# Output and slope rows by one generator, turned loads of d h behind the loads of h, and a scratch row moved, in a kernel for an S4 convolution with a gated feed-forward and its gradients

## The chip, the cores and the metric

The kernel runs on one core of a Trainium2 chip. The metric is the device time of one execution in microseconds (us). The engines of the core run side by side, each with its own list of instructions: TensorE (PE, matmuls; PEld is its weight load), VectorE (DVE), ScalarE (ACT), GpSimd (POOL) and SyncE (SP). SP here issues nearly all loads and part of the stores, POOL issues most of the other stores, and ACT a few. A DMA waits on its issuing engine until what it needs is there, so a DMA that must wait holds up every later one of the same engine.

## What is computed

With L = 2048 rows, D = 512 columns, F = 1792 hidden units and N = 128 states, in bf16:

```python
xn = layernorm(x)                       # over the 512 columns
K  = real(sum_n C[d,n] * exp(dt*A)[d,n]^l * dt*B[d,n])
s  = irfft(rfft(xn, 2L) * rfft(K, 2L))[:L] + xn * Dskip
h  = xn @ w1;   z = silu(h) @ w2;   g = silu(z)
out = x + s * g
```

Wanted are `out` (out_0) and the gradients for a given gradient r of `out`: of x (out_1), of A, B, C (real and imaginary, out_2 to out_7), of log_dt and Dskip (out_8, out_9), of w1 (out_10) and of w2 (out_11). The backward needs, row by row, d z = r * s * silu'(z) (called the slope rows here, kept in `k.do`), then d a = d z @ w2^T, d h = d a * silu'(h), the part of d xn that comes from d h @ w1^T (called Pd), d w2 = silu(h)^T d z, d w1 = xn^T d h, and at the end the backward of the norm, which adds Pd, the convolution's part dU and r.

## The kernel before

Everything is cut in blocks of 128 x 128. The 2048 rows are 16 tiles, and a *chunk* is two of them, 256 rows. The convolution goes through a Fourier transform made of matmuls, in four blocks of 128 columns. What doesn't stay on the chip goes to DRAM scratch and comes back: `Sd` the rows of s (one block of columns after the other), `Gd` the gate g, `Hd` the rows of h (turned: hidden units on the partitions), `DHd` the same for d h, `Ud` and `KXd` spectra, `Pd`, `dUd`.

The work is written as Python generators, and the order in which they are advanced is the order of the program. There are these stages:

1. Norm, tables and the forward of the convolution beside the feed-forward (`chain`, `gen_ffn_fwd`).
2. A stretch whose order for PE, ACT and DVE is written by hand as a string of letters. Among them G makes the gate rows and stores them to Gd, W makes the turned weights (`W1`, `W2`), L and M make the slope rows of chunks 0 and 1 (`gen_slope_rows(..., True)`). After it, "BB A BB A" begins the backward.
3. `paced(bwd, woven([ffb, out], [2, 1]), BR)`: the backward of the convolution (`gen_conv_bwd`, by columns, with the spectra as `sp_in` of 1 MB), and beside it two steps of `gen_ffn_da` for one of `gen_out`. This and all that follows is ordered by a scheduler; buffers (`bufs=`) and order decide what waits.
4. The gradients of the states (`gen_ssm_bwd`; loads `YT`, `Eb`, `GE`, `par_*`; tiles `ps_v`, `psS`, `gout`) beside the rest of `gen_ffn_da`, and then beside `gen_dw2`.
5. `interleave([gen_ln_bwd, dw])`: the backward of the norm beside the rest of `gen_dw2` and `gen_dw1`.

What the change touches, and the names to follow:

- `gen_ffn_da`, for each chunk: load h in two halves (`dhT`, of 8 and 6 hidden blocks, from Hd) and put silu' over it at once (ACT, L962); d z turned (`doT`); seven groups of 8 matmuls (`ps_da`, L989) with the product on DVE (L991); the store of d h to DHd (SP, L994); then `ps_dx` (L1000) with the copy to `pd_s` by ACT and its store to Pd (SP, L1003). At f == 2 it asks for slope rows two chunks ahead (`k.slopes`, `k.later`).
- The slope rows of chunks 2 to 7: a second instance of `gen_slope_rows` in a pool of its own ("late"), with loads of Sd (`S`) and of r (`Gs`), a silu' on ACT (L675) and two products on DVE (L678, L680).
- `gen_out`, chunks 0 to 7: loads of Sd (`go_s`) and Gd (`go_g`) two chunks ahead, a load of x (`go_x`, L707) in the chunk's own step, the products L709 and L710 on DVE, the store of out_0 by POOL.
- `gen_dw2`, for each of 14 hidden blocks: load `h_in` (128 x 2048, 512 KB, L1012; two buffers), turn it on PE (`pt_t`, L112; 16 matmuls), silu on ACT to `a_tok` (L1017), 16 matmuls `ps_w2` (L1032), copy to `o11` and store.
- `gen_dw1`, for each of 7 pairs of hidden blocks: two transposing DMAs of DHd to `dh_tok` (512 KB each, L1045; three buffers of a pair each), 4 x 16 matmuls `ps_w1` (L1050), copy to `o10` and store. In the profile `ps_w1` and `ps_w2` are both called ps_w, and o1, o10 and o11 are called o. As the buffers of dh_tok are free early, the scheduler puts the first six of its transposes on SP among the loads of `gen_dw2` and of the states.
- `gen_ln_bwd`, for each chunk: loads `du`, `pd_l`, `Gt` (SP, L1069 to L1073; four buffers), sums on DVE (L1082, and L1083 which writes its product to a scratch row `jk`), ACT, and `o1` (L1093, L1094), stored by POOL to out_1.

## Time and profile before

| | |
|---|---|
| Median of 3 runs | 687.6 us (687.19 to 688.8) |
| Profiled execution, its own time | 690.33 us |
| Span in its profile, first to last instruction | 688.4 us |
| Mean granted TensorE clock | 0.958 |
| Busy: PE, DVE, ACT | 600.2, 515.4, 455.3 us |
| DMA | 148.41 MB, mean 216 GB/s |

The profile has a page and views of the trace. In a timeline a row is: start in us, duration, engine, line, operation, output <- input by the program's names, shape, count (consecutive instructions are grouped), and in brackets the engine's idle time ahead of it with what ended it. A row of waits is: engine, what waited, what for, the sum in us, the number of times, the longest. A row of windows is: the stretch, then busy time of PE, PEld, DVE, ACT, POOL (with instructions), the granted clock of TensorE as a share of full speed, the mean busy share of the 16 DMA engines, and GB/s. SPq is SP's queue. A time comes from one execution, so it is compared with that execution's own time.

### The profile page before, as it was taken

The numbers are of one execution on the slowest core, as the hardware profiler recorded it, in microseconds if no ns is written. First come the engines' busy times: TensorE is split into PE (matmuls) and PEld (weight loads), VectorE is DVE, ScalarE is ACT, GpSimd is POOL, SyncE is SP. The second block draws the span as 40 slices with busy tenths as digits, with TensorE's granted clock in tenths as the row PEclk, the third lists the DMA queues.
The fourth block names the chain that finished last, engine by engine and source line by source line (L and its number), as shares of the span: only waits on it lengthen the run. The fifth ranks groups of instructions, "written<-read, shape, count | busy, mean of one in ns | idle before, by whom it ended". The sixth has DMA issues, their size and how long they took to land. (4 is left out here: it accounts for less than half of the span.)

```text
span 688.4 us, 14482 instructions
## 1 busy us (share of the span) xinstructions
PE 600.2 (87%) x5884; PEld 436.6 (63%) x5884; DVE 515.4 (75%) x917; ACT 455.3 (66%) x613; POOL 86.4 (13%) x172
## 2 busy tenths in 40 slices
PE   0687998999999977889789999989989969999798
PEld 0445665776675755657475866757677747766677
DVE  6979999899695789887687959537596753945880
ACT  6869779997969777857465775515677744634431
POOL 2354101010100120000000000000002020023211
PEclk9989999999999999899899999999999998999989
DMA  9955556846566787789777446469999996344994
GB/s 287 341 151 211 196 167 250 285 171 230 176 232 226 280 270 264 240 256 304 222 224 231 147 161 203 134 138 235 242 230 243 199 239 184 97 156 158 271 253 119
DMA packets 158018, 148.41 MB, mean 216 GB/s; under 512 B 79552, under 2 KB 134592, under 8 KB 154368
## 3 DMA queue, kind: packets, MB, share of 16 engines
q1 hardware_dynamic: 148640, 124.67, 63.6%
q0 software_dynamic: 6768, 19.93, 8.0%
q10 hardware_dynamic: 2544, 2.88, 1.3%
q8 instruction: 46, 0.75, 0.5%
q14 instruction: 20, 0.16, 0.1%
HBM read 65.01 MB, written 62.00 MB: 185 GB/s over the span
## 5 line engine op out<-in xcount | busy, mean ns | idle before, releaser
L45 ACT CAST dA<-ps_s 128x1024 bf16<-128x1024 f32 x89 | 87.2, 1031 | 10.0 <-PE ps_s L301 6.7
L832 DVE TENSOR_TENSOR Tp<-Vb,Eb 128x1344 bf16<-128x1344 bf16 x64 | 52.1, 854 | 25.7 <-issue 11.1
L989 PE MATMUL ps_da<-doT,W 128*128 128x256 bf16 x448 | 64.8, 288 | 3.2 <-DVE dhT L991 3.2
L615 PE MATMUL ps_o<-W,aT 128*128 128x512 bf16 x224 | 59.5, 396 | 5.5 <-ACT aT L607 3.2
L599 PE MATMUL ps_h<-XT,W 128*128 128x256 bf16 x448 | 61.7, 281 | 1.4 <-ACT hT L45 0.6
L45 ACT CAST dB<-ps_i 128x1024 bf16<-128x1024 f32 x47 | 46.0, 1032 | 23.0 <-PE ps_i L341 23.0
L341 PE MATMUL ps_i<-I,sp_in 128*128 128x256 bf16 x384 | 51.3, 281 | 8.8 <-DVE sp_in L374 4.7
L991 DVE TENSOR_TENSOR dhT<-ps_da,dhT 128x512 bf16<-128x512 f32 x56 | 38.0, 686 | 27.2 <-PE ps_da L989 20.8
L1050 PE MATMUL ps_w<-dh_tok,xn 128*128 128x256 bf16 x448 | 52.1, 281 | 4.0 <-DMA dh_tok<-DHd 4.0
L45 ACT CAST o<-ps_w 128x256 bf16<-128x256 f32 (+1 forms) x42 | 18.4, 442 | 54.4 <-PE ps_w L1050 23.9
L1000 PE MATMUL ps_dx<-W,dhT 128*128 128x512 bf16 x224 | 54.2, 383 | 0.0
L989 PEld LDWEIGHTS <-W 128*128 128x128 bf16 x448 | 44.3, 104 | 15.2 <-issue 7.9
L45 ACT CAST Vb<-ps_v 128x672 bf16<-128x672 f32 x64 | 42.4, 725 | 15.2 <-PE ps_v L822 15.2
L1032 PE MATMUL ps_w<-YD,a_tok 128*128 128x512 bf16 x224 | 52.3, 379 | 0.0
L1050 PEld LDWEIGHTS <-xn 128*128 128x128 bf16 x448 | 45.0, 101 | 11.2 <-issue 4.5
L599 PEld LDWEIGHTS <-W 128*128 128x128 bf16 x448 | 42.8, 101 | 13.7 <-issue 6.8
L341 PEld LDWEIGHTS <-sp_in 128*128 128x128 bf16 x384 | 36.9, 100 | 21.9 <-DVE sp_in L374 7.7
L301 PEld LDWEIGHTS <-TF 128*128 128x128 bf16 x384 | 27.1, 103 | 20.9 <-issue 13.9
L615 PEld LDWEIGHTS <-aT 128*128 128x128 bf16 x224 | 20.6, 101 | 30.4 <-issue 8.0
L46 DVE COPY dB<-pt_f 128x2048 bf16<-128x2048 bf16 x24 | 28.5, 1219 | 12.9 <-PE pt_f L310 12.7
L1000 PEld LDWEIGHTS <-dhT 128*128 128x128 bf16 x224 | 21.6, 99 | 22.6 <-issue 2.0
L45 ACT CAST hT<-ps_h 128x512 bf16<-128x512 f32 x56 | 32.3, 613 | 4.5 <-PE ps_h L599 4.5
(231 smaller groups left out, 1283.5 us busy)
## 6 DMA issues: line engine op xcount, KB each, us to landing
Yd<-YD SPq DMA_DIRECT2D x8, 1024.0 KB, 4.3
sp_in<-Ud SPq DMA_DIRECT2D x8, 1024.0 KB, 7.4
h_in<-Hd SPq DMA_DIRECT2D x14, 512.0 KB, 5.1
Ed<-E SPq DMA_DIRECT2D x8, 672.0 KB, 3.6
Eb<-Ed SPq DMA_DIRECT2D x8, 672.0 KB, 5.4
Hd<-hT POOLq DMA_DIRECT2D x8, 512.0 KB, 5.6
Ud<-dA SPq DMA_DIRECT2D x4, 1024.0 KB, 4.8
KXd<-dA SPq DMA_DIRECT2D x4, 1024.0 KB, 5.4
```

The costliest lines, as they stand in the source:

```text
L45: return self.nc.scalar.copy(out=out, in_=in_)
L46: return self.nc.vector.tensor_copy(out=out, in_=in_)
L301: nc.tensor.matmul(out=ps[:, j], lhsT=k.TF[:, 8 * h + j, c, :], rhs=U(8 * h + j), start=True, stop=True)
L341: nc.tensor.matmul(out=ps[:, g], lhsT=Y[:, c, g0 + g, :], rhs=k.I2[:, c].rearrange("p c m -> p (c m)"), start=(c == 0), stop=(c == 1))
L599: nc.tensor.matmul(out=ps[:, j], lhsT=k.W1[:, dk, ft * P:ft * P + P], rhs=XTv[:, :, dk, :], start=(dk == 0), stop=(dk == DK - 1))
L615: nc.tensor.matmul(out=ps[:], lhsT=aT[:, ft, t * P:t * P + P], rhs=k.W2[:, ft, :], start=(ft == 0), stop=(ft == FT - 1))
L832: k.nc.vector.tensor_tensor(out=Tp[:, c, :, r ^ c].rearrange("p e (q w) a -> p q w e a", w=2), in0=Vb[:, :, c].rearrange("p q w (e a) -> p ...
L989: nc.tensor.matmul(out=ps[:, j], lhsT=k.W2[:, ft, dk * P:dk * P + P], rhs=dTv[:, :, dk, :], start=(dk == 0), stop=(dk == DK - 1))
L991: nc.vector.tensor_tensor(out=dh[:, i0:i0 + 2, :], in0=ps[:], in1=dh[:, i0:i0 + 2, :], op=ALU.mult)
L1000: nc.tensor.matmul(out=ps[:], lhsT=dhs[ft // 8][:, ft % 8, t * P:t * P + P], rhs=k.W1[:, :, ft * P:ft * P + P], start=(ft == 0), stop=(ft ...
L1032: nc.tensor.matmul(out=ps[:], lhsT=at[:, t, :], rhs=k.do[:, t, :], start=(t == 0), stop=(t == k.T - 1))
L1050: nc.tensor.matmul(out=ps[:], lhsT=k.xn[:, t, dk * P:dk * P + P], rhs=dh[:, t].rearrange("p j n -> p (j n)"), start=(t == 0), stop=(t == k ...
```

## The change

- The slope rows of chunks 2 to 7 move from the late `gen_slope_rows` into `gen_out`, in a pool of its own ("go"). One load of Sd (`go_s`) serves slope and output of a chunk. r is loaded as `go_r`, x as `go_x` in three buffers and two chunks ahead with the others. The chunks go 2 to 7, then 0 and 1, and `gen_out` is finished ahead of the states' gradients.
- In `gen_ffn_da` the silu' of dhT is issued apart from its load, at f == 2 and f == 6; the check on slope rows moves from f == 2 to f == 4; pd_s gets two buffers.
- In `gen_dw1` the transposes of dh_tok are issued behind the last load of h_in. In the changed program all six first ones stand in a row on SP, behind that load and ahead of the loads of the norm.
- The scratch row jk moves from the norm's pool to the pool of the weights' gradients. o11 gets three buffers, o1 four.

In the changed program's own order, further: five loads of dhT stand on SP ahead of the spectra and the first loads of `gen_out`, with three silu' of dhT among ACT's copies of the turned weights; DVE does slope and output of chunks 4 and 5 one after the other; the last two turns and four of dw2's blocks of 16 matmuls remain on PE behind the last h_in load's release, with the states' psS matmuls ahead of it (before, two rounds of psS stood behind it).

```diff
@@ gen_slope_rows @@
-def gen_slope_rows(k, pool, chunks, early):
+def gen_slope_rows(k, pool, chunks):
...
-        n = 3 if early else 4
...
-        if early:
-            Gr = k.Gr[:, ts, :]
-        else:
-            G = pool.tile([P, 2, k.D], BF16, name="Gs", tag="Gs", bufs=2)
-            nc.sync.dma_start(G[:], k.g_v[:, ts, :])
-            Gr = G[:]
...
-def gen_out(k, pool):
+def gen_out(k, pool, early):
 
     nc = k.nc
     TT = nc.vector.tensor_tensor
@@ -696,21 +683,40 @@
         ts = slice(2 * c, 2 * c + 2)
         S = pool.tile([P, 4, 2, P], BF16, name="go_s", tag="go_s", bufs=2)
         nc.sync.dma_start(S[:].rearrange("p b t d -> p b (t d)"), k.Sd[:, :, 256 * c:256 * c + 256].rearrange("b p n -> p b n"))
+        G = None
+        if c >= early:
+            G = pool.tile([P, 2, k.D], BF16, name="go_r", tag="go_r", bufs=2)
+            nc.sync.dma_start(G[:], k.g_v[:, ts, :])
         g = pool.tile([P, 2, k.D], BF16, name="go_g", tag="go_g", bufs=2)
         nc.sync.dma_start(g[:], k.Gd[:, ts, :])
-        return S, g
-    q = [load(0), load(1)]
-    yield
-    for c in range(n):
-        S, g = q.pop(0)
-        x = pool.tile([P, 2, k.D], BF16, name="go_x", tag="go_x", bufs=1)
-        nc.sync.dma_start(x[:], k.x_v[:, 2 * c:2 * c + 2, :])
+        x = pool.tile([P, 2, k.D], BF16, name="go_x", tag="go_x", bufs=3)
+        nc.sync.dma_start(x[:], k.x_v[:, ts, :])
+        return S, G, g, x
+
+    def slope(c, G):
+        if G is not None:
+            with k.tc.issue_after(k.mark):
+                nc.scalar.activation(out=k.do[:, 2 * c:2 * c + 2, :], in_=k.do[:, 2 * c:2 * c + 2, :], func=ACT.Derivative_silu)
+    q = [load(early), load(early + 1)]
+    yield
+    slope(early, q[0][1])
+    order = list(range(early, n)) + list(range(early))
+    for i, c in enumerate(order):
+        S, G, g, x = q.pop(0)
+        yield
+        if G is not None:
+            o = k.do[:, 2 * c:2 * c + 2, :]
+            TT(out=o, in0=o, in1=G[:], op=ALU.mult)
+            TT(out=rows(o), in0=rows(o), in1=S[:], op=ALU.mult)
+            k.slopes = c + 1
+        if q:
+            slope(order[i + 1], q[0][1])
         yield
         TT(out=rows(g[:]), in0=rows(g[:]), in1=S[:], op=ALU.mult)
         TT(out=x[:], in0=x[:], in1=g[:], op=ALU.add)
         k.st(k.o0_v[:, 2 * c:2 * c + 2, :], x[:])
-        if c + 2 < n:
-            q.append(load(c + 2))
+        if i + 2 < n:
+            q.append(load(order[i + 2]))
         yield
 
 
@@ -959,12 +965,15 @@
         c, f0, n = halves[i]
         dh = da.tile([P, n, 256], BF16, name="dhT", tag="dhT%d" % n, bufs=3 if n == 8 else 2)
         nc.sync.dma_start(dh[:, 0:n], k.Hd[f0:f0 + n, :, 256 * c:256 * c + 256].rearrange("f p n -> p f n"))
-        nc.scalar.activation(out=dh[:, 0:n], in_=dh[:, 0:n], func=ACT.Derivative_silu)
         return dh
+
+    def slope(dh):
+        nc.scalar.activation(out=dh[:], in_=dh[:], func=ACT.Derivative_silu)
     for c in range(T // 2):
         if c == 0:
             dN = turned_rows(k, da, k.do, 0, "doT", k.evb)
             ahead = [load(0)]
+            slope(ahead[0])
             yield
         dT = dN
         dTv = dT[:].rearrange("p (t k) n -> p t k n", k=DK)
@@ -976,11 +985,13 @@
                 i = 2 * c + f // 4 + 1
                 if i < len(halves):
                     ahead.append(load(i))
-            if f == 2:
+            if f == 4:
                 while k.slopes < min(c + 3, T // 2):
                     next(k.later)
             if f == 4 and c + 1 < T // 2:
                 dN = turned_rows(k, da, k.do, c + 1, "doT", k.evb)
+            if f in (2, 6) and ahead:
+                slope(ahead[0])
             i0 = 2 * (f % 4)
             ps = k.pf.tile([P, 2, 256], F32, name="ps_da", tag="pf")
             for j in range(2):
@@ -994,7 +1005,7 @@
                 nc.sync.dma_start(k.DHd[f0:f0 + n, :, 256 * c:256 * c + 256].rearrange("f p n -> p f n"), dh[:, 0:n])
             yield
         for t in range(2):
-            pd = da.tile([P, D], BF16, name="pd_s", tag="pd_s", bufs=1)
+            pd = da.tile([P, D], BF16, name="pd_s", tag="pd_s", bufs=2)
             ps = k.pf.tile([P, D], F32, name="ps_dx", tag="pf")
             for ft in range(FT):
                 nc.tensor.matmul(out=ps[:], lhsT=dhs[ft // 8][:, ft % 8, t * P:t * P + P], rhs=k.W1[:, :, ft * P:ft * P + P],
@@ -1009,7 +1020,7 @@
 
     def load(ft):
         h = fw.tile([P, k.T, P], BF16, name="h_in", tag="h_in", bufs=2)
-        nc.sync.dma_start(h[:].rearrange("p t n -> p (t n)"), k.Hd[ft])
+        k.h_in = nc.sync.dma_start(h[:].rearrange("p t n -> p (t n)"), k.Hd[ft]).ins
         return h
 
     def turn(h):
@@ -1030,7 +1041,7 @@
         ps = k.pf.tile([P, k.D], F32, name="ps_w2", tag="pf")
         for t in range(k.T):
             nc.tensor.matmul(out=ps[:], lhsT=at[:, t, :], rhs=k.do[:, t, :], start=(t == 0), stop=(t == k.T - 1))
-        ob = fw.tile([P, k.D], BF16, name="o11", tag="o11", bufs=2)
+        ob = fw.tile([P, k.D], BF16, name="o11", tag="o11", bufs=3)
         k.evb(ob[:], ps[:])
         k.st(k.outs[11][ft * P:ft * P + P, :], ob[:])
         yield
@@ -1041,8 +1052,9 @@
     o10 = k.outs[10].rearrange("(k p) f -> p k f", p=P)
     for f in range(k.FT // 2):
         dh = fw.tile([P, k.T, 2, P], BF16, name="dh_tok", tag="dh_tok", bufs=3)
-        for j in range(2):
-            nc.sync.dma_start_transpose(dh[:, :, j, :], k.DHd[2 * f + j])
+        with k.tc.issue_after(k.h_in):
+            for j in range(2):
+                nc.sync.dma_start_transpose(dh[:, :, j, :], k.DHd[2 * f + j])
         ob = fw.tile([P, k.DK, 256], BF16, name="o10", tag="o10", bufs=2)
         for dk in range(k.DK):
             ps = k.pf.tile([P, 256], F32, name="ps_w1", tag="pf")
@@ -1078,9 +1090,8 @@
         m = lw.tile([P, 2, 4], F32, name="m", tag="m", bufs=2)
         for i in range(2):
             t = 2 * c + i
-            jk = lw.tile([P, D], BF16, name="jk", tag="jk", bufs=1)
             STT(out=cols(pd[:, i]), in0=cols(pd[:, i]), scalar=1.0, in1=du[:, :, i, :], op0=ALU.mult, op1=ALU.add, accum_out=m[:, i, 0:1])
-            STT(out=jk[:], in0=pd[:, i], scalar=1.0, in1=k.xn[:, t, :], op0=ALU.mult, op1=ALU.mult, accum_out=m[:, i, 1:2])
+            STT(out=k.jk[:], in0=pd[:, i], scalar=1.0, in1=k.xn[:, t, :], op0=ALU.mult, op1=ALU.mult, accum_out=m[:, i, 1:2])
         STT(out=m[:, :, 2:4], in0=m[:, :, 0:2], scalar=-1.0 / D,
             in1=k.rstd[:, 2 * c:2 * c + 2].unsqueeze(2).to_broadcast([P, 2, 2]), op0=ALU.mult, op1=ALU.mult)
         for i in range(2):
@@ -1088,7 +1099,7 @@
         return pd, Gt, m
 
     def rows(c, pd, Gt, m):
-        o1 = lw.tile([P, 2, D], BF16, name="o1", tag="o1", bufs=2)
+        o1 = lw.tile([P, 2, D], BF16, name="o1", tag="o1", bufs=4)
         for i in range(2):
             STT(out=o1[:, i], in0=k.xn[:, 2 * c + i, :], scalar=m[:, i, 3:4], in1=Gt[:, i], op0=ALU.mult, op1=ALU.add)
         TT(out=o1[:], in0=o1[:], in1=pd[:], op=ALU.add)
@@ -1225,7 +1236,7 @@
     k.g, k.mark = [], None
     early = range(2)
     streams = {"C": gen_conv_fwd(k, 3), "F": ffn, "G": gen_gate_rows(k, gp), "H": gen_ds_rows(k), "B": bwd,
-               "W": chained([gen_turned(k, k.W1, evw), gen_turned(k, k.W2, evw)]), "L": gen_slope_rows(k, gp, early[0:1], True), "M": gen_slope_rows(k, gp, early[1:], True)}
+               "W": chained([gen_turned(k, k.W1, evw), gen_turned(k, k.W2, evw)]), "L": gen_slope_rows(k, gp, early[0:1]), "M": gen_slope_rows(k, gp, early[1:])}
     ordered = ctx.enter_context(ExitStack())
     ordered.enter_context(tc.manual_schedule(engines={mybir.EngineType.PE, mybir.EngineType.Activation, mybir.EngineType.DVE}))
     for s in "GGG F GG F WWW CC W G C W C C W C HH GG C W C CC F C G L CC W C G HH L CC WW L HH C MM WW C L C HH WW MM".replace(" ", ""):
@@ -1238,25 +1249,25 @@
     turn = itertools.chain(["w8"] * 2, itertools.cycle(["w8"] * 2 + ["w8b"] * 2 + ["w8"] * 2))
     k.dftb.tile = lambda shape, dt, name, tag: base.tile(shape, dt, name=name, tag=next(turn) if tag == "w8" else tag)
     da = pool("da", es=es_d)
-    es_l = es_d.enter_context(ExitStack())
-    k.later = gen_slope_rows(k, pool("late", es=es_l), range(len(early), 8), False)
-    out = gen_out(k, da)
+    k.slopes = len(early)
+    es_o = es_d.enter_context(ExitStack())
+    out = k.later = gen_out(k, pool("go", es=es_o), len(early))
     ffb = gen_ffn_da(k, da)
     for s in "BB A BB A".replace(" ", ""):
         next({"A": ffb, "B": bwd}[s], None)
     ordered.close()
     k.mark = next(i for i in reversed(nc.cur_bb.bb.instructions) if i.engine == mybir.EngineType.Activation)
     paced(bwd, woven([ffb, out], [2, 1]), BR)
-    run(k.later)
-    es_l.close()
+    run(out)
+    es_o.close()
     es_x.close()
     es_b = ctx.enter_context(ExitStack())
     sb = pool("sb", side="right", es=es_b)
     ssm = gen_ssm_bwd(k, sb)
     paced(ffb, ssm, SR)
-    run(out)
     es_d.close()
     fw = pool("fw")
+    k.jk = fw.tile([P, D], BF16, name="jk")
     dw = chained([gen_dw2(k, fw), gen_dw1(k, fw)])
     paced(ssm, dw, 0.35)
     es_b.close()
```

20 lines of the change are left out of this document (7 added, 13 removed).

## The prediction

> **What bounds the kernel now.** I read the page first, then TensorE's and the other engines' waits from 296 us on (where the change begins to act), then the timelines of the places where those waits lie, engine by engine, and last the queue of SP near the end.
>
> ```profile
> span 688.4 us, 14482 instructions
> ...
> PE 600.2 (87%) x5884; PEld 436.6 (63%) x5884; DVE 515.4 (75%) x917; ACT 455.3 (66%) x613; POOL 86.4 (13%) x172
> ...
> PEclk9989999999999999899899999999999998999989
> ```
>
> TensorE is busy 87% of the span, so what a change can win is the idle time of PE and the half-clock stretch that follows an idle one (the slices marked 8). Nothing in the diff adds or removes a matmul. The windows show where the idle is: the columns are PE, PEld, DVE, ACT, POOL, then the granted clock, the DMA share and GB/s.
>
> ```profile
> 300.00:320.00 20.00, 16.24 (x172) 13.46 (x170) 17.16 (x24) 15.78 (x16) 1.08 (x2) 0.91 0.86 261
> 320.00:340.00 20.00, 16.71 (x107) 8.77 (x105) 10.63 (x17) 9.96 (x13) 1.08 (x2) 0.83 0.88 270
> 340.00:360.00 20.00, 16.57 (x173) 13.95 (x171) 18.04 (x26) 12.56 (x13) 1.08 (x2) 0.91 0.72 215
> ...
> 560.00:580.00 20.00, 14.02 (x123) 10.47 (x122) 3.93 (x6) 6.94 (x11) 4.23 (x8) 0.83 0.87 227
> ```
>
> The waits from 296 to 690 us (total, times, longest), one row for each resource that the change touches:
>
> ```profile
> PE pt_t L112 <- DMA h_in<-Hd: 6.8, 3, 6.0
> ...
> PE ps_s L301 <- DVE du_b L754: 2.0, 2, 1.0
> PE ps_s L301 <- ACT dA L45: 1.8, 2, 1.3
> PE ps_s L322 <- ACT dA L45: 1.3, 1, 1.3
> ...
> DVE go_x L710 <- DMA go_x<-in_A_u_dram: 15.8, 5, 6.1
> ...
> ACT pd_s L45 <- DMA Pd<-pd_s: 7.4, 3, 2.7
> ...
> SPq L707 <- DMA out_dram<-go_x: 22.8, 7, 6.0
> ```
>
> VectorE waits 15.8 us for x rows, because SP may not load the next x tile until the store of the last output has landed (22.8 us of SP). ScalarE waits 7.4 us for the single pd_s tile. TensorE waits once for 6.0 us for an h_in.
>
> **Part 1: x rows three times buffered, pd_s twice.** ScalarE, VectorE and TensorE in the stretch:
>
> ```profile
> 299.54 1.48 ACT L962 ACTIVATE dhT<-dhT 128x1536 bf16<-128x1536 bf16 x1 [3.81 <-DMA dhT<-Hd]
> ...
> 305.48 0.58 ACT L45 CAST pd_s<-ps_dx 128x512 bf16<-128x512 f32 x1 [2.15 <-DMA Pd<-pd_s]
> ```
> ```profile
> 326.61 0.69 DVE L710 TENSOR_TENSOR go_x<-go_x,go_g 128x1024 bf16<-128x1024 bf16 x1 [3.30 <-DMA go_x<-in_A_u_dram]
> ...
> 340.10 0.69 DVE L710 TENSOR_TENSOR go_x<-go_x,go_g 128x1024 bf16<-128x1024 bf16 x1 [6.13 <-DMA go_x<-in_A_u_dram]
> ```
> ```profile
> 307.03 2.37 PE L341 MATMUL ps_i<-I,sp_in 128*128 128x256 bf16 x16 [2.28 <-ACT dA L45]
> 309.19 2.98 PE L989 MATMUL ps_da<-doT,W 128*128 128x256 bf16 x14
> 312.01 1.91 PE L341 MATMUL ps_i<-I,sp_in 128*128 128x256 bf16 x16
> ...
> 329.69 0.61 PE L341 MATMUL ps_i<-I,sp_in 128*128 128x256 bf16 x2 [3.29 <-DVE sp_in L374]
> ...
> 330.51 3.19 PE L341 MATMUL ps_i<-I,sp_in 128*128 128x256 bf16 x14
> ...
> 344.89 1.47 PE L989 MATMUL ps_da<-doT,W 128*128 128x256 bf16 x12
> ```
>
> Place one, 305 to 312: ScalarE first waits 3.81 us for dhT and then 2.15 for pd_s, and dA comes 2.28 us late to PE; behind it sixteen ps_i take 2.37 instead of 1.91 and fourteen ps_da 2.98 where 14/12 of 1.47 is 1.72. 2.28 + 0.46 + 1.26 = 4.0 us. Place two, 326 to 334: the go_x wait of 3.30 stands ahead of VectorE's sp_in products, PE idles 3.29, and fourteen ps_i take 3.19 instead of 14/16 of 1.91, 1.67: 3.29 + 1.52, with the slow pair after the idle some 5 us. Place three, 340 to 351: the go_x wait of 6.13 comes back as two idles for du_b (2.0) and one for dA (1.3), 3.3 us, and the window's clock of 0.91 (9% of 20 us) adds about 1: 4.3. That is 13.3 us if every wait goes and nothing comes instead.
>
> It can't all go, since VectorE does no less there (the same two slope and two output products of 0.69 us for each chunk). In 300 to 360 it works 17.16 + 10.63 + 18.04 = 45.8 us. The fullest window, 340:360, has it at 18.04 of 20, 90%; 45.8/0.9 is 50.9, so the 60 us shrink by at most 9.1. I take 9, bounds 0 and 13.3. Later, the pd_s wait that costs PE 1.3 us (ps_s L322) goes with the second pd_s tile: 1.
>
> Also here: six of the fourteen late loads of Sd (256 KB each) vanish, as one load serves slope and output, which takes work from a DMA share of 0.72 to 0.88; and splitting the derivative from the load lets five dhT loads go out on SP ahead of the spectra (1 MB each) and the first rows, with three derivatives placed among ScalarE's weight copies ahead of doT. If such a load is late, ScalarE stands still with its copies behind it: between nothing and the 3.81 us that it waited for a dhT at 299.54. I take nothing, as the copies give the loads more time than they had, and keep 3.81 for the range. The check on slopes moved from f == 2 to f == 4 issues nothing itself.
>
> **Part 2: the dh_tok transposes leave the h_in loads alone.** SP and TensorE:
>
> ```profile
> 552.35 4.42 SPq L1045 DMA_TRANSPOSE dh_tok<-DHd  x1
> 556.87 0.52 SPq L804 DMA_DIRECT2D Eb<-Ed  x1
> 557.44 4.39 SPq L1045 DMA_TRANSPOSE dh_tok<-DHd  x1
> ...
> 563.27 0.52 SPq L1012 DMA_DIRECT2D h_in<-Hd  x1
> ```
> ```profile
> 568.48 0.71 PE L112 MATMUL pt_t<-ident,h_in 128*128 128x128 bf16 x5 [5.98 <-DMA h_in<-Hd]
> ```
>
> Two transposes hold SP for 8.8 us just ahead of the h_in for which PE then idles 5.98 us. In the changed program no dh_tok stands there, so the h_in goes out that much earlier and the idle goes. The window 560:580 has a clock of 0.83, and with 14.02 us of PE work in it the slow part costs about 2 more. I take 7.5 of the 8, bounds 5 and 8. Sum of the gains: 9 + 1 + 7.5 = 17.5 us.
>
> **Part 3: what the same move costs at the end.** All six first transposes now stand on SP in one block behind the last h_in and ahead of all loads of the norm (du, pd_l, Gt). The seventh transpose stands behind the du of the norm's chunk 6, whose buffer (one of four) is freed by VectorE's L1082 sum of chunk 2. So the chain is: six transposes, the first du, the norm's first chunks, the seventh transpose, dw1's fourth step on PE. The rows:
>
> ```profile
> L1045 SPq DMA_TRANSPOSE dh_tok<-DHd x14: 2022/3942/5677, 529.1 to 671.4; - x14
> ```
> ```profile
> DMA to landing us min/median/max: 2.8/5.7/6.1
> ```
> ```profile
> 638.38 5.07 SPq L1045 DMA_TRANSPOSE dh_tok<-DHd  x1
> ...
> 659.85 15.17 SPq L1045 DMA_TRANSPOSE dh_tok<-DHd  x4
> ```
> ```profile
> 630.58 0.69 DVE L1083 SCALAR_TENSOR_TENSOR jk<-pd_l,xn 128x512 bf16<-128x512 bf16 x1 [6.13 <-DMA out_dram<-gout]
> ...
> 637.19 0.69 DVE L1082 SCALAR_TENSOR_TENSOR pd_l<-pd_l,du 128x512 bf16<-128x512 bf16 x1
> ```
> ```profile
> 620.79 1.06 PE L112 MATMUL pt_t<-ident,h_in 128*128 128x128 bf16 x16
> ...
> 622.85 6.65 PE L1032 MATMUL ps_w<-YD,a_tok 128*128 128x512 bf16 x30
> 629.33 21.12 PE L1050 MATMUL ps_w<-dh_tok,xn 128*128 128x256 bf16 x192
> 654.42 31.00 PE L1050 MATMUL ps_w<-dh_tok,xn 128*128 128x256 bf16 x256 [3.96 <-DMA dh_tok<-DHd]
> ```
>
> Let H be the moment at which the last h_in is issued. Four transposes in a row took 15.17 us, 3.79 each, so six end at H + 22.8. The first du lands 5.7 us (median of that tile, the landing row) after its issue: H + 28.5. The norm then needs two L1082 of 0.69 (1.3) and, from 630.58 to the end of the pair at 637.9, 7.3 us more: H + 37.1, and the seventh transpose goes out at about H + 37.5. In the trace it goes out at 638.38 and the fourth step of dw1 starts at 654.42, 16.0 us later: H + 53.5. What PE has by then: in the changed program's order 64 dw2 matmuls (6.65/30 = 0.222 each, 14.2) and two turns of 1.06 stand between H and dw1, 16.3 us, and the first three steps take 21.1: done at H + 37.4. PE idles 16.1 us where it idled 3.96: a loss of 12.1. The first three dh_tok pairs are no trouble (the first lands by about H + 14, needed at H + 16.3), and the tail behind the fourth step stays as it was, as the same transposes and norm loads share SP.
>
> Bounds by the transpose row: at its least, 2.02 us, six take 12.1 and the loss is 1.4; at its most, 5.68, they take 34.1 and the loss is 23.4. I take the 3.79 of the back-to-back four, since these six are back to back as well.
>
> The Trainium skill bears on this price ("DMA: Bandwidth & Descriptors", section Latency and other measured facts): it gives 261 GB/s as the rate of a DMA transpose with a non-contiguous middle dimension. A 512 KB transpose would take 2.0 us by it, an estimate from that page, and the sum at the tail would be a loss of about 1.4 us; the four in a row at 3.79 us do not agree with it, the shortest of the fourteen does.
>
> **Part 4: the norm's scratch row and o buffers.** The 6.13 us idle ahead of the first jk at 630.58 (its memory was still being stored as gout) goes. By itself it frees the chain 630.58 to 637.9, but the new chain starts later than that anyhow, so I count nothing for it; if part 3's block is quicker than I think, it is already in the sums, which start the norm without this wait. o1 in four and o11 in three buffers: nothing, PE has no wait of its own on either.
>
> **The sum.** -17.5 + 12.1 = -5.4 us on the profiled execution's own 690.33, so 684.9. That execution is 2.7 above the median of 687.6; the same difference taken from the median gives 682.
>
> **The rivals.**
> - *The block is short.* If the six transposes take 2.0 to 3 us each with nothing of SP's between them, the loss is 1 to 7 and the time 671 to 677; 671.5 at 2.0. For it: the 2022 of the row; against: the four at the end took 3.79. Chance 0.15. The transpose rate of "DMA: Bandwidth & Descriptors" in the Trainium skill is the rule that leads here.
> - *The block is long, and the kernel slower.* Place: SP behind the last h_in. Each 1 us more on a transpose is 6 us on the end. The gain of 17.5 is used up at 3.79 + 5.4/6 = 4.7 us each; at 5.68 the loss is 23.4 and the time 687.6 + 5.9 = 693.5. For it: 5.07 at 638.38, and the maximum of the row; against: the median of 3.94. Chance 0.22.
> - *The loads ahead don't come ahead.* go_g and go_s still have two buffers, and SP is one queue in order: a load two chunks ahead may stand behind a store that waits for VectorE, and slope and output of a chunk now wait together for one set of loads, with the sp_in products behind them on VectorE. Then places one to three keep their 9 us in another name, the gain is 8.5, and the time 687.6 - 8.5 + 12.1 = 691. For it: SP's own waits; against: the 22.8 us on landed stores, the cause of the late x, can't recur with three tiles. Chance 0.13.
> - The forecast, 677 to 686: chance 0.5.
>
> **How the numbers follow.** A measurement of this kernel tells some 0.2%, 1.4 us, from no change. Faster takes 0.44 of the forecast's 0.5 and 0.14 of the short block: 0.58. About the same takes 0.04 of the forecast, 0.01 of the short block and 0.02 of the long one, around its break-even: 0.07. Slower takes 0.02 of the forecast, 0.20 of the long block and the 0.13 of the third: 0.35. The range, from 669 (short block with the whole 13.3 in part 1 would give 667) to 695 (long block, and 1.5 of the dhT wait), leaves out the ends of both.
>
> **What would show it.** In the profile after: go_x waits of VectorE in 298 to 345 gone and 320:340 back near full clock; no wait of PE for h_in above 1 us; six transposes in a row on SP behind the last h_in, and PE's wait for dh_tok, with the norm's VectorE work idle ahead of it, at 12 to 20 us instead of 3.96. I am wrong in part 1 if PE's idle in 300 to 360 only changes its releaser (go_g, sp_in), in part 2 if an h_in wait of several us stays, in part 3 if the dh_tok wait stays below 8 us or goes beyond 25.

## The result and the profile after

| | before | changed |
|---|---|---|
| Median | 687.57 us | 677.92 us |
| Lowest to highest | 687.19 to 688.8 | 676.74 to 681.53 |
| Profiled execution, its own time | 690.33 us | 678.5 us |
| Span in the profile | 688.4 us | 676.7 us |

The ratio is 0.9866, with a 95% interval of 0.9826 to 0.9905: 9.65 us faster, where 5.6 was forecast (682.0, range 669 to 695). A second series (e5 below) gave 0.9855 (0.9802 to 0.9909).

The page of the changed kernel: PE's share of the span is the same 87%, because its busy time fell by as much as the span, 600.2 to 588.7 us against 688.4 to 676.7. Some of that fall is only missing records (5849 of 5884 matmuls); e5, the same kernel with all 5884, has 592.3 us of 681.1. So PE's idle time in sum hardly changed (88.2 us before, 88.8 in e5): the same matmuls took less time, and the mean granted clock rose from 0.958 to 0.970 (0.972 in e5).

```profile
span 676.7 us, 14442 instructions
...
PE 588.7 (87%) x5849; PEld 431.7 (64%) x5884; DVE 515.3 (76%) x917; ACT 455.3 (67%) x613; POOL 86.1 (13%) x172
...
PEclk9879999999999999798999999989999999998989
```

The windows in which the first part acts (PE, PEld, DVE, ACT, POOL, granted clock, DMA share, GB/s), and its waits from 296 us on:

```profile
300.00:320.00 20.00, 17.10 (x180) 14.29 (x178) 15.75 (x23) 12.46 (x13) 0.54 (x1) 0.91 0.75 236
320.00:340.00 20.00, 17.66 (x137) 10.39 (x135) 16.71 (x25) 11.20 (x14) 2.16 (x4) 0.95 0.91 290
340.00:360.00 20.00, 19.45 (x201) 16.02 (x199) 19.14 (x28) 14.76 (x17) 1.09 (x2) 0.97 0.39 129
```
```profile
PE ps_w L1062 <- DMA dh_tok<-DHd: 5.2, 1, 5.2
...
PE ps_w L1062 <- ACT o L45: 3.4, 2, 3.1
...
DVE YD L709 <- DMA go_r<-in_grad_out_dram: 2.7, 1, 2.7
...
SPq L693 <- DMA out_dram<-go_x: 6.1, 3, 3.4
```

From 296 to 380 us, ScalarE's two longest waits for dhT and PE's waits of over 2 us:

```profile
307.87 1.48 ACT L971 ACTIVATE dhT<-dhT 128x1536 bf16<-128x1536 bf16 x1 [2.76 <-DMA dhT<-Hd]
...
372.87 3.29 ACT L971 ACTIVATE dhT<-dhT 128x1536 bf16<-128x1536 bf16 x2 [3.64 <-DMA dhT<-Hd]
```
```profile
310.30 0.27 PE L341 MATMUL ps_i<-I,sp_in 128*128 128x256 bf16 x1 [2.51 <-ACT dB L45]
...
337.60 0.74 PE L301 MATMUL ps_s<-ds,TF 128*128 128x128 bf16 x8 [2.27 <-DVE du_b L760]
...
377.10 0.61 PE L301 MATMUL ps_s<-ds,TF 128*128 128x128 bf16 x8 [3.01 <-ACT dA L45]
```

VectorE works 51.6 us of these 60 instead of 45.8 and PE 54.2 instead of 49.5. No go_x row is left among VectorE's waits; go_r has 2.7 us in its place. PE has no wait for h_in. PE's waits in this stretch are fewer but not gone: twice a silu' on ScalarE waits for a late dhT, the copy behind it (dB, dA) is late, and PE waits 2.51 and 3.01 us for that copy. SP still waits 6.1 us for landed stores (22.8 before), as the third x buffer only comes free when its store has landed.

At the end: SP, VectorE, ScalarE and PE.

```profile
593.13 0.32 SPq L1023 DMA_DIRECT2D h_in<-Hd  x1
593.50 16.82 SPq L1057 DMA_TRANSPOSE dh_tok<-DHd  x6
610.75 0.38 SPq L1081 DMA_DIRECT2D du<-dUd  x1
...
625.76 5.31 SPq L1057 DMA_TRANSPOSE dh_tok<-DHd  x1
```
```profile
616.74 0.69 DVE L1093 SCALAR_TENSOR_TENSOR pd_l<-pd_l,du 128x512 bf16<-128x512 bf16 x1 [13.12 <-DMA pd_l<-Pd]
```
```profile
613.65 0.37 ACT L45 CAST o<-ps_w 128x256 bf16<-128x256 f32 x1 [1.12 <-PE ps_w L1062]
620.13 1.52 ACT L1098 ACTIVATE pd_l<-pd_l,m,rstd 128x512 bf16<-128x512 bf16 x2 [6.11 <-DVE m L1095]
621.55 0.35 ACT L45 CAST o<-ps_w 128x256 bf16<-128x256 f32 x1
```
```profile
611.70 7.15 PE L1062 MATMUL ps_w<-dh_tok,xn 128*128 128x256 bf16 x64
621.95 12.13 PE L1062 MATMUL ps_w<-dh_tok,xn 128*128 128x256 bf16 x96 [3.10 <-ACT o L45]
634.33 3.65 PE L1062 MATMUL ps_w<-dh_tok,xn 128*128 128x256 bf16 x32 [0.25 <-ACT o L45]
643.14 30.74 PE L1062 MATMUL ps_w<-dh_tok,xn 128*128 128x256 bf16 x256 [5.15 <-DMA dh_tok<-DHd]
```

The six transposes stand in a row behind the last h_in, and VectorE idles 13.12 us for the norm's first rows. ScalarE shows a wait that the prediction did not have: a copy of dw1's sums (o) stands in its order behind the norm's scaling of pd_l, which waits 6.11 us for VectorE's m, and PE waits 3.10 us for that copy.

**How the runs below are compared.** In every kernel the same matmuls stand ahead of dw1's first one, and the same 448 behind it. So two numbers tell where the time went: when dw1 starts (the first start in the row of dh_tok), and how long the program goes on after that (span less that start). A third is PE's busy time in 300 to 360 us (the sum row of the windows). There is one profile of each, not all on the same chip (e1 to e4 shared one, e5 to e11 another, e12 ran on a third); the ratio is against runs of the kernel before on the same chip. Ratios are taken over fast runs alone, and so need not be the quotient of the medians given below, which count every run; only in e6 one run of 1118.12 us, with a granted clock of 0.887, is left out of the median too. A profile is one execution: those of e3, e5, e6, e7, e9 and e10 were the slowest of their runs, 5.2, 1.8, 3.8, 3.1, 3.3 and 4.2 us above the median, and that of e8 the fastest, 3.2 below it.

| run | ratio (95%) | dw1 starts | rest | PE in 300:360 |
|---|---|---|---|---|
| before | | 629.3 | 59.1 | 49.5 |
| changed | 0.9866 (0.9826 to 0.9905) | 611.7 | 65.0 | 54.2 |
| e1 dh_tok free | 0.9901 (0.985 to 0.9952) | 619.2 | 57.4 | 53.3 |
| e2 dh_tok's rule alone | 0.9919 (0.9868 to 0.997) | 618.4 | 61.6 | 49.3 |
| e3 dh_tok spread | 0.9864 (0.9776 to 0.9953) | 616.2 | 62.9 | 53.6 |
| e4 one go_x | 0.9897 (0.9858 to 0.9935) | 613.7 | 64.7 | 52.8 |
| e5 changed, again | 0.9855 (0.9802 to 0.9909) | 616.7 | 64.4 | 53.0 |
| e6 five dh_tok, spread | 0.9712 (0.9645 to 0.9779) | 616.1 | 56.1 | 53.7 |
| e7 one pd_s | 0.9864 (0.9807 to 0.9922) | 616.2 | 66.4 | 54.1 |
| e8 silu' at the load | 0.99 (0.9838 to 0.9962) | 613.5 | 64.7 | 51.4 |
| e9 generator alone | 0.9892 (0.9858 to 0.9927) | 624.5 | 63.6 | 48.1 |
| e10 silu' split alone | 1.0011 (0.9966 to 1.0056) | 629.1 | 67.4 | 50.4 |
| e11 dh_tok free, norm undone | 0.9856 (0.9799 to 0.9913) | 623.0 | 59.6 | 55.0 |
| e12 before with e6's tail | 0.979 (0.9745 to 0.9835) | 620.7 | 54.0 | 47.7 |

The starts of dw1 of one and the same kernel differ by 5 us (changed: 611.7 and 616.7), so a difference of 2 or 3 us in one profile says nothing. PE's busy time also counts slow matmuls in full, so it is the roughest of the three. Every interval but that of e10 lies below 1; among themselves most overlap, and only e6's lies wholly below that of the changed kernel.

### The profile page after: what moved, and what is told of

It is laid out like the page before. It is cut to its first block, busy times and chain, and to the rows that moved or that the text cites. A ratio compares the mean times of both kernels' runs of the same rounds, so it can differ in the third digit from the quotient of the medians.

```text
span 676.7 us, 14442 instructions
## 1 busy us (share of the span) xinstructions
PE 588.7 (87%) x5849; PEld 431.7 (64%) x5884; DVE 515.3 (76%) x917; ACT 455.3 (67%) x613; POOL 86.1 (13%) x172
## 4 chain that ended last, share of the span: by engine, by line
PE 37%; DVE 28%; ACT 14%; DMA 10%; SPq 5%; issue 4%; POOL 0%; ACTq 0%; DVEq 0%; POOLq 0%
PE ps_w L1043 5%; PE ps_w L1062 5%; PE ps_dx L1011 4%; DMA dhT<-Hd 3%; PE ps_da L1000 3%; PE ps_o L615 3%; ACT sn L463 3%; SPq L1057 2%; PE ps_i L341 2%; PE ps_s L322 2%; DVE sp_in L373 2%; PE psS L854 2%; ACT dA L45 2%; PE ps_s L301 2%; DVE dB L46 2%
## 5 line engine op out<-in xcount | busy, mean ns | idle before, releaser
L599 PE MATMUL ps_h<-XT,W 128*128 128x256 bf16 x448 | 62.9, 285 | 1.3 <-DVE XT L46 0.6
L1000 PE MATMUL ps_da<-doT,W 128*128 128x256 bf16 x448 | 61.4, 282 | 0.6 <-DVE dhT L1002 0.2
L1062 PE MATMUL ps_w<-dh_tok,xn 128*128 128x256 bf16 x448 | 53.7, 285 | 8.6 <-DMA dh_tok<-DHd 5.2
L615 PE MATMUL ps_o<-W,aT 128*128 128x512 bf16 x203 | 53.3, 388 | 6.8 <-ACT aT L607 3.4
L45 ACT CAST dB<-ps_i 128x1024 bf16<-128x1024 f32 x47 | 46.2, 1034 | 16.1 <-PE ps_i L341 15.2
L1062 PEld LDWEIGHTS <-xn 128*128 128x128 bf16 x448 | 45.8, 102 | 16.5 <-DMA dh_tok<-DHd 5.4
L1043 PE MATMUL ps_w<-YD,a_tok 128*128 128x512 bf16 x211 | 48.5, 379 | 0.7 <-issue 0.2
L1043 PEld LDWEIGHTS <-a_tok 128*128 128x128 bf16 x224 | 21.1, 98 | 22.9 <-issue 0.4
```

Source lines behind the costliest of these rows:

```text
L45: return self.nc.scalar.copy(out=out, in_=in_)
L599: nc.tensor.matmul(out=ps[:, j], lhsT=k.W1[:, dk, ft * P:ft * P + P], rhs=XTv[:, :, dk, :], start=(dk == 0), stop=(dk == DK - 1))
L615: nc.tensor.matmul(out=ps[:], lhsT=aT[:, ft, t * P:t * P + P], rhs=k.W2[:, ft, :], start=(ft == 0), stop=(ft == FT - 1))
L1000: nc.tensor.matmul(out=ps[:, j], lhsT=k.W2[:, ft, dk * P:dk * P + P], rhs=dTv[:, :, dk, :], start=(dk == 0), stop=(dk == DK - 1))
L1043: nc.tensor.matmul(out=ps[:], lhsT=at[:, t, :], rhs=k.do[:, t, :], start=(t == 0), stop=(t == k.T - 1))
L1062: nc.tensor.matmul(out=ps[:], lhsT=k.xn[:, t, dk * P:dk * P + P], rhs=dh[:, t].rearrange("p j n -> p (j n)"), start=(t == 0), stop=(t == k ...
```

## The experiments: the move of dh_tok

**e1, the changed kernel with dh_tok free.**

```diff
-        with k.tc.issue_after(k.h_in):
-            for j in range(2):
-                nc.sync.dma_start_transpose(dh[:, :, j, :], k.DHd[2 * f + j])
+        for j in range(2):
+            nc.sync.dma_start_transpose(dh[:, :, j, :], k.DHd[2 * f + j])
```

> The changed kernel without the rule that dh_tok goes behind the last h_in; all else stays. The trace of the changed kernel has dw1 starting 17.6 us earlier than before and its fourth step only 11.3 us earlier, so the tail gives back 6.3 us. Theory A (the move is a gain of about 7.5 us at the h_in wait and a loss of about 6.3 at the tail): a wait of PE for h_in of 4 to 8 us comes back, the norm starts some 17 us sooner after the last h_in, PE's wait for dh_tok ahead of the fourth step of dw1 goes from 5.2 to under 4, and the time is 677.9 + 7.5 - 6.3 = 679, between 676 and 682. Rival B (the move is where the change gains): 684 to 688. Rival C (the move only loses, the h_in wait of before was a matter of the order around it): 671 to 673.

678.92 us against 690.08 of the kernel before: 0.9901. PE:

```profile
555.57 0.49 PE L112 MATMUL pt_t<-ident,h_in 128*128 128x128 bf16 x5 [2.38 <-DMA h_in<-Hd]
...
619.16 21.12 PE L1061 MATMUL ps_w<-dh_tok,xn 128*128 128x256 bf16 x192
641.40 12.55 PE L1061 MATMUL ps_w<-dh_tok,xn 128*128 128x256 bf16 x112 [1.11 <-DMA dh_tok<-DHd]
```

An h_in wait is back, of 2.4 us and not the 4 to 8 expected; dw1 starts at 619.2, where e4 of the same chip, with the rule (and one buffer for go_x), has 613.7. In return dw1's first three steps run through in 21.1 us and the rest takes 57.4 instead of 64.7. Gain and loss of the move cancel to 2 us, as theory A has it. Rival C is out. The interval, 677 to 684 us when put on the kernel before's 687.6, just touches the lower end of rival B, but the longer rest with the rule speaks against it.

**e2, the rule alone, in the kernel before.** The same edit the other way round, with `k.h_in` set at the load.

> The kernel before with only the rule that dh_tok is issued behind the last h_in. Theory A: the 6.0 us wait for h_in goes, the six transposes in a row move the norm's loads back by 17 us, and the time is 687.6 - 7.5 + 6.3 = 686.4, between 684 and 689. Rival B: 678 to 681. Rival C: 692 to 694.

684.19 against 690.08, 0.9919. The time is inside A's 684 to 689, but the kernel before was slower here than the 687.6 that A counts from; 0.9919 of 687.6 is 682, between A and B. The wait for h_in is gone; all of PE's waits from 540 us on:

```profile
PE ps_w L1051 <- DMA dh_tok<-DHd: 7.2, 3, 3.9
```

dw1 starts 10.9 us earlier than in the kernel before (629.3 to 618.4), and the rest grows from 59.1 to 61.6. So in the kernel before the move is worth more than in the changed one: its h_in wait was 6.0 us, in e1 2.4. The tail's loss is small here, 2.5 us, but see e10 for how far one profile's tail can be trusted.

**e3, three pairs spread between the last loads of h_in.**

```diff
+        k.h_ins = getattr(k, "h_ins", []) + [k.h_in]
...
-        with k.tc.issue_after(k.h_in):
+        with k.tc.issue_after(k.h_ins[(9, 10, 11, 13)[min(f, 3)]]):
```

> The changed kernel with the first three pairs of dh_tok behind the 10th, 11th and 12th load of h_in (of 14) instead of the last, so that they lie between the last h_in loads, where the DMA share of the changed kernel is 0.37 to 0.50, and the norm's loads follow the last h_in at once. Theory A: no wait for h_in comes back, the norm's first sum comes some 6 to 10 us after the last h_in instead of 23.6, dw1's first three steps take 21 instead of 26.3 us and the wait ahead of the fourth goes to 0 to 4: 677.9 - 6.3 - 0 to 4 = 668 to 672. Rival (SP is full there too, and the h_in loads wait behind the transposes as they did before): 676 to 682, with a wait of PE for h_in over 3 us.

675.79, 0.9864; the profiled execution took 681.02, the other three 672.43 to 676.49. The first half came as expected: no h_in wait, dw1's first three steps in 21.1 us. The rest nevertheless took 62.9 us:

```profile
639.64 15.76 PE L1063 MATMUL ps_w<-dh_tok,xn 128*128 128x256 bf16 x128 [2.30 <-DMA dh_tok<-DHd]
660.76 15.44 PE L1063 MATMUL ps_w<-dh_tok,xn 128*128 128x256 bf16 x128 [5.36 <-DMA dh_tok<-DHd]
```
```profile
645.27 17.56 SPq L1058 DMA_TRANSPOSE dh_tok<-DHd  x4
```
```profile
640.00:660.00 20.00, 15.40 (x128) 12.97 (x125) 11.28 (x27) 5.70 (x13) 3.89 (x6) 0.93 1.20 226
```

The norm is early now, and in this execution PE waits all the same, further on, for the last eight transposes, with a DMA share of 1.20 (it sums the times of packets, and can pass 1). The 668 to 672 of theory A was not reached, and in this profile these waits are why. Whether the eight transposes are held by the DMA engines, which they share with the norm's loads and stores, or by SP's queue, in which they stand among them, this run does not tell; e6 takes transposes out of both.

**e6, five pairs ahead of the tail.** Five buffers, the pairs behind the 9th to 13th load of h_in, and room made for them (the list k.h_ins as in e3; the tile k.jk goes).

```diff
-        dh = fw.tile(..., name="dh_tok", tag="dh_tok", bufs=3)
-        with k.tc.issue_after(k.h_in):
+        dh = fw.tile(..., name="dh_tok", tag="dh_tok", bufs=5)
+        with k.tc.issue_after(k.h_ins[(8, 9, 10, 11, 12, 13)[min(f, 5)]]):
...
-        ob = fw.tile([P, k.D], BF16, name="o11", tag="o11", bufs=3)
+        ob = fw.tile([P, k.D], BF16, name="o11", tag="o11", bufs=2)
...
-            STT(out=k.jk[:], in0=pd[:, i], scalar=1.0, in1=k.xn[:, t, :], ...)
+            STT(out=du[:, :, i, :], in0=cols(pd[:, i]), scalar=1.0, in1=cols(k.xn[:, t, :]), ...)
```

> The changed kernel with five buffers for dh_tok and the first five pairs behind the 9th to 13th load of h_in, one pair each, so that only four transposes are left for the tail. Room for it: o11 back to two buffers, and the norm's scratch product goes into the du tile that has been used up. Theory A (the tail is bound by the transposes that are left and the norm's loads and stores on the same DMA engines, and the stretch ahead of it has room): PE's waits for dh_tok go to under 2 us, the stretch from the start of dw1 to the end takes 51 to 54 us (68.9 in the changed kernel, 57.7 with dh_tok set free), and the time is 6 to 9 us under the changed kernel of this run. Rival (the DMA engines are as full ahead of the tail): PE waits for h_in by 3 us or more, and the time is that of the changed kernel within 3 us.

670.38, 0.9712, where the changed kernel beside it has 681.05. SP and PE:

```profile
579.07 7.21 SPq L1058 DMA_TRANSPOSE dh_tok<-DHd  x2
586.40 0.52 SPq L1023 DMA_DIRECT2D h_in<-Hd  x1
586.96 6.65 SPq L1058 DMA_TRANSPOSE dh_tok<-DHd  x2
593.73 0.51 SPq L1023 DMA_DIRECT2D h_in<-Hd  x1
```
```profile
616.10 29.86 PE L1063 MATMUL ps_w<-dh_tok,xn 128*128 128x256 bf16 x272
647.14 3.65 PE L1063 MATMUL ps_w<-dh_tok,xn 128*128 128x256 bf16 x32 [1.18 <-ACT o L45]
653.43 15.88 PE L1063 MATMUL ps_w<-dh_tok,xn 128*128 128x256 bf16 x144 [2.64 <-ACT o L45]
```

A pair fits between two h_in loads, PE waits for none of them, and it has no wait for dh_tok at all; what is left is ScalarE's copy behind the norm. The rest takes 56.1 us, 8.3 less than in e5 beside it, and dw1 starts where it did. Theory A's mechanism holds, and its numbers are missed by a little: the rest is 2 us longer than the 51 to 54 expected, and the time 10.7 us less where 6 to 9 were. (The expectation's 68.9 for the changed kernel's rest is a slip; it is 65.0.) Of the parts of this edit, the order, the two more buffers and the used du tile, only the order was tried alone, for three pairs (e3).

**e12, the same tail in the kernel before.**

> The kernel before with only the tail of the fastest kernel so far: dh_tok in five buffers behind the 9th to 13th load of h_in, o1 in four buffers, the norm's scratch product in the used du tile; the convolution's backward stays as it was. If the two parts of the change are independent, this takes the h_in wait (some 9 us of PE's loss in the trace of before) and most of the tail's 5 to 8 us, and leaves the 3 to 7 us of the convolution's backward: 0.978 to 0.985 of the kernel before, where the same tail on the changed kernel had 0.971. If the tail's gain needs the earlier part: 0.99 to 1.0.

677.01 against 690.36: 0.979, as independent parts would have it. Its row of dw1:

```profile
620.67 35.10 PE L1052 MATMUL ps_w<-dh_tok,xn 128*128 128x256 bf16 x320
```

The first part's stretch is as in the kernel before (47.7 us of PE in 300:360), dw1 starts at 620.7 (the h_in wait is gone here too) and the rest takes 54.0. This edit of dh_tok and the norm alone is worth as much as the whole change, and likely more: 0.979 (0.9745 to 0.9835) against 0.9866 (0.9826 to 0.9905).

**e11, dh_tok free and the norm's parts undone** (jk in the norm's pool, o1 in two buffers).

> The changed kernel with dh_tok set free, as in an earlier run, and the norm's parts undone: jk in the norm's pool again, o1 in two buffers. There the norm's loads follow the last h_in at once, so the scratch row can matter. The prediction counted it at nothing because the norm was late anyway. If the scratch row matters once the norm is early: VectorE's first L1094 product waits 4 to 6 us for the stores of gout, the seventh transpose goes out as much later, and the tail from the start of dw1 to the end takes 60 to 64 us instead of 57.7. If not: 57 to 59.

684.75, 0.9856. VectorE's waits:

```profile
DVE jk L1094 <- DMA out_dram<-gout: 5.4, 1, 5.4
```

The wait for the stores of gout is back. The rest takes 59.6 us against 57.4 in e1: 2 us, just below the 60 to 64 expected and no more than two profiles differ. That the scratch row matters once the norm is early is likely, and not shown.

## The experiments: the convolution's backward

**e4, one go_x** (`bufs=3` to `bufs=1` for the tile go_x).

> The changed kernel with one buffer for go_x instead of three. Theory A (the wait of x on the landed store is what held VectorE and through it TensorE in 300 to 360): VectorE's waits for go_x of 3 to 6 us come back, PE loses 5 to 9 us there, 683 to 687. Rival (the gain there comes from the loads of dhT issued early, pd_s and one load of Sd instead of two): 677 to 680.

680.07, 0.9897. Waits of VectorE, then PE:

```profile
DVE go_x L716 <- DMA go_x<-in_A_u_dram: 10.2, 3, 5.2
```
```profile
PE ps_s L301 <- DVE du_b L760: 5.3, 2, 3.4
```
```profile
sum 60.00, PE 52.81 PEld 40.46 DVE 51.91 ACT 38.75 POOL 3.77; mean PE 17.60 PEld 13.49 DVE 17.30 ACT 12.92 POOL 1.25
```

Ten us of go_x waits are back, and PE loses nearly nothing by them: 52.8 us busy in 300:360 (53.0 to 54.2 in the changed kernel) and dw1 at 613.7. 680.07 lies at the upper end of the rival and below theory A: in this company the late x rows cost TensorE nothing that this profile can tell. By the ratio a loss of some us is not excluded (0.9897 against 0.9866 and 0.9855).

**e7, one pd_s** (`bufs=2` to 1), and **e8, the silu' of dhT at its load** (and the check at f == 2).

> The changed kernel with one pd_s buffer instead of two. One buffer for x changed nothing in the run before, so what made the convolution's backward 5 to 9 us shorter must be pd_s, the dhT loads ahead of their silu', or the single load of Sd and r for slope and output. If it is pd_s: ScalarE's waits for the store of pd_s (4.8 us before) come back and the stage from the first ps_da to the end of the convolution's backward takes 3 to 5 us longer than in the changed kernel of this run. If not: within 1.5 us of it.

> The changed kernel with the silu' of dhT issued with its load again, and the check on slope rows back at f == 2. If the early loads of dhT carry the gain of the convolution's backward: ScalarE's waits for dhT go back to some 10 us and the stage takes 4 to 8 us longer than in the changed kernel of this run. If they don't: within 1.5 us of it, and what is left as the cause is that slope and output share one generator and one load.

ScalarE's waits, in e7 and in e8:

```profile
ACT pd_s L45 <- DMA Pd<-pd_s: 4.0, 2, 3.9
```
```profile
ACT dhT L968 <- DMA dhT<-Hd: 13.3, 5, 5.4
```

Each wait is back in its kernel, and dw1 starts no later for it: 616.2 and 613.5 against 616.7 for the changed kernel beside them. The stage that the expectations name (from the first ps_da to the last inverse-transform matmul, L353) takes 149.1 us in e7 and 151.6 in e8 against 152.1. The medians are 0.4 and 2.5 us above the changed kernel's 681.05, the ratios 0.9864 and 0.99 against 0.9855, with overlapping intervals. So neither loses the 3 to 8 us expected of a cause, but e8's 2.5 us lie between the two expectations. e8's PE has 51.4 us in 300:360, some 2 less than the changed kernel, which it makes up later.

**e9, all three undone at once**, so that only the one generator with its single load of Sd is left, with the rule for dh_tok and the norm's parts.

> The changed kernel with one go_x, one pd_s and the silu' of dhT at its load and the check at f == 2, all three undone at once; left of the first part is the one generator with its single load of Sd. Each of the three undone alone left the gain of the convolution's backward in place. Theory D (slope and output in one generator carry it: six loads of Sd less, and the output's products no longer stand among the spectra's on VectorE while x is late): TensorE loses 15 to 19 us between 300 and 360 as in the changed kernel's runs (21 to 24 in the kernel before), and the time is within 2 us of the changed kernel's 681 where the kernel before has 692. Rival (the three cover for one another, any one is enough): the loss is back at 21 to 24 us, and the time at 685 to 690.

686.52, 0.9892, on the chip of e5, where the kernel before took 693.38 this time. The waits, the sum of the three windows, PE's longest wait in them and its first row of dw1:

```profile
DVE go_x L716 <- DMA go_x<-in_A_u_dram: 17.9, 4, 8.5
```
```profile
ACT pd_s L45 <- DMA Pd<-pd_s: 7.5, 3, 5.7
```
```profile
sum 60.00, PE 48.13 PEld 35.04 DVE 45.07 ACT 32.72 POOL 2.71; mean PE 16.04 PEld 11.68 DVE 15.02 ACT 10.91 POOL 0.90
```
```profile
348.81 1.01 PE L301 MATMUL ps_s<-ds,TF 128*128 128x128 bf16 x8 [6.79 <-DVE du_b L760]
...
624.50 7.15 PE L1057 MATMUL ps_w<-dh_tok,xn 128*128 128x256 bf16 x64
```

PE is at 48.1 us there, below the kernel before, and dw1 starts at 624.5, 8 to 11 us behind the kernels with one of the three undone. The ratio is near that of the rule for dh_tok alone (0.9919 in e2), so no gain of the one generator by itself shows. Theory D is out by its own number: the time is 5.5 us above the changed kernel's 681.05 and not within 2. (Its 15 to 19 and 21 to 24 us are not counted as in the table, where 60 less PE's busy time gives 11.9 here and 10.5 before.) The three together carry most of the gain of the convolution's backward. That they cover for one another, any two of them being enough, is what the starts of dw1 say. The times allow another reading: the medians of e7 and e8 are 0.4 and 2.5 us above the changed kernel's, e4's ratio is some 3 us above e5's, and three such small losses added up come to about the 5.5 us of e9. This profile is e9's slowest run, its stage of 154.3 us is only 3 to 5 longer than in the kernels with one undone, and no two were undone together. Which of the two readings is right stays open.

**e10, the silu' split alone, in the kernel before.**

> The kernel before with only the silu' of dhT issued apart from its load and the check moved to f == 4. Theory D: ScalarE's waits for dhT fall from 9.9 to 3 to 8 us, but VectorE still waits some 14 us for x rows, and the time is within 2 us of the kernel before. Rival: 4 to 7 us faster than the kernel before.

694.17 against 693.38, 1.0011: no difference, as theory D expected; its rival, 4 to 7 us faster, is out. But the waits are not those expected. ScalarE's for dhT are 14.7 us, not 3 to 8, and VectorE's:

```profile
DVE go_g L709 <- DMA go_g<-Gd: 7.1, 2, 5.6
...
DVE go_x L710 <- DMA go_x<-in_A_u_dram: 2.4, 2, 1.5
```

The wait for the output's rows goes by the name of go_g here (2.4 us before); why was not followed up. So this one of the three, alone and in the kernel before, shows no gain, within some 3 us. The other two were not tried alone. The tail of this run, whose order on SP is that of the kernel before, took 67.4 us against 59.1, with 10.4 us of waits for dh_tok; in 640:660 it moved 244 GB/s where the first profile of the kernel before moved 279. That window of before, and then of e10:

```profile
640.00:660.00 20.00, 16.04 (x123) 13.02 (x122) 18.08 (x49) 8.39 (x16) 3.68 (x6) 0.83 1.14 279
```

```profile
640.00:660.00 20.00, 15.46 (x127) 12.93 (x126) 17.96 (x47) 8.14 (x16) 3.69 (x6) 0.91 1.13 244
```

## Why the prediction was right, point by point

The direction and the places came out as forecast: gains in the convolution's backward and at the h_in wait, a part of them given back at the tail. The sizes did not. Gains and loss were both put too high, by some 3 and by 5 to 6 us, and in the net the two errors partly cancel; that 677.92 lies within the forecast's 677 to 686 is in part luck. The prediction took 1.4 us as what a measurement can tell; over more runs the kernel before spread from 681.33 to 691.41 us on one chip. And PE's idle time, of which most of the sum is made, hardly changed in all: what went ahead of dw1 came back in the tail (7.0 us idle there before, 12.2 in e5) and between.

- **The gains, 17.5 us.** In the first profile dw1 starts 17.6 us earlier (629.33 to 611.70). That agreement is better than the parts deserve. Over all runs dw1 starts at 614.4 (changed, e4, e5, e7, e8: 611.7, 613.7, 616.7, 616.2, 613.5) against 629.2 (before and e10): 14.8.
- **Part 1, 9 + 1.** With the rule for dh_tok in both, 619.6 (e2, e12) goes to 614.4: 5 us; without it, 629.2 goes to 621.1 (e1, e11): 8 us. So 5 to 8, below the 10 taken. VectorE got fuller than the 90% taken as its ceiling (19.14 of 20 in 340:360), so the bound of 9.1 was not a hard one, but the gain stayed under it. Of the three places named, place two lost PE's wait (3.29 us) whole, place three went from 3.3 to 2.27, and place one only changed its releaser: 2.28 us for dA before, 2.51 for dB after. That is the late dhT load which the prediction named and put at nothing: ScalarE waited 2.76 us for it with dB behind it, and once more at 372.87, where PE lost 3.01 us, so the 1 us from the second pd_s tile did not come either. One cause for each place was also too simple: x buffers (e4) or pd_s (e7) could go alone without a loss that the traces show, and all three together bring the stall back (e9). Whether they cover for one another or add up is open, as said there.
- **Part 2, 7.5.** 629.2 to 619.6 in the kernel before (9.6), 621.1 to 614.4 in the changed one (6.7). The mechanism holds, and the size in the kernel before. In the changed one the wait itself was only 2.4 us without the rule (e1; 3.0 in e11), so more than half of the 6.7 is not traced to it and may be spread of the profiles.
- **Part 3, a loss of 12.1.** Measured: 5.9 (59.1 to 65.0), 7.3 between e1 and e4 on one chip. This is the term that was mis-sized, and by the prediction's own sign part 3 was wrong: PE's wait for dh_tok was 5.15 us, below the 8 it had set. The six transposes took 16.82 us, 2.80 each, not 3.79: the row of four at the end was taken because they stand back to back too. Those four run beside the norm's loads and stores, the six do not; that this makes the difference is argued from the traffic and was not tested by itself. From there the chain ran as drawn: du issued 17.6 us after the last h_in, first sum at 23.6 (28.5 forecast), seventh transpose at 32.6 (37.5), fourth step of dw1 at 50.0 (53.5).
- **What the sum did not have.** PE's wait ahead of the fourth step was only 5.15 us instead of 16.1, but the first three steps took 26.3 us instead of 21.1, as ScalarE's copies stood behind the late norm (3.10 us, and a clock of 0.91 in 620:640). 10.3 us against 3.96 is the loss of 6.3. Of the 5.8 us less than the 12.1 forecast, 3.5 are the earlier fourth step and 2.3 that dw1 started 18.6 us after the last h_in, not 16.3.
- **The rivals.** The short block (0.15) is the one whose condition came true: the six transposes took 2.80 us each, between 2 and 3. In the prediction's own sum that price gives a loss of 6.1 us and a time of 676, closer than the forecast's 682. The rate of 261 GB/s in the Trainium skill ("DMA: Bandwidth & Descriptors", Latency and other measured facts), an estimate of 2.0 us each, lies below what these six took, 2.80, and far below the four at the end of e3, 4.39 each; the measurement decides. The long block did not come. The third rival (the loads ahead don't come ahead) is seen in small: go_r took 2.7 us of VectorE.
- **Part 4** at nothing: not refuted; e11 lets it be 2 us.

## What to carry to other kernels

Where several waits end near one another, undo each change alone, in pairs and all together: here each of three alone cost little or nothing, all three 5.5 us, and without the pairs it stays open whether they cover for one another or add up. A load with other work behind it in an engine's list needs a price: the late dhT loads, put at nothing, cost PE 2.51 and 3.01 us. A load that must leave a crowded place is best put into the next place with room (in e6 one pair of transposes between two loads of h_in, with the buffers to hold them), and not behind the last one: the queue behind it pays. Price a transfer by a row that has the same company: six transposes in a row took 2.80 us each where four in a row beside the norm's loads and stores took 3.79, though that the company makes the difference is argued and not shown.

## What the runs showed of the hardware

- How long a transpose of 512 KB holds SP is no constant: between 1.3 and 6.9 us among the fourteen of e6, 2.80 each for six in a row in the changed kernel. The row of e6 (least, median, most in ns):

```profile
L1058 SPq DMA_TRANSPOSE dh_tok<-DHd x14: 1332/3967/6910, 559.3 to 642.9; - x14
```

- One and the same tail, with the same order on SP, took 59.1 us in the profile of the kernel before and 67.4 in that of e10, with the rate in 640:660 at 279 and 244 GB/s. e10's profile is the slowest of its ten runs. What makes the DMA slower there stays open.
